# Attention and linear attention on one core: packed odd and even heads for the out-projection, paced projections, inserted zero products, 32-row scores, and transposing loads

## The chip, the cores and the metric

The kernel runs on one core of one Trainium2 chip. The metric is the device time of one execution in microseconds (us). The clock in this text is the share of its full clock that TensorE (PE) was granted. "Fast" and "slow" are states of runs: a run on one core is called slow when it is over 1.5% above the fastest of the same kernel. Ratios are the mean time of one kernel's fast runs over that of the kernel before in the same rounds, so they are not quite ratios of the medians that I quote.

## The reference

Two independent attentions over 2048 tokens, width 512, 32 heads of 16, side by side in the output.

```python
# A: softmax attention
q, k, v = split(x @ wqkv)                        # 32 heads, 16 wide
p = softmax(q @ k^T / 4)                         # 32 x 2048 x 2048
a = (p @ v) @ wo
# B: linear attention
phi(t) = [softmax(t @ w_phi), softmax(-t @ w_phi)]     # 32 features a head
kv, z = phi(k)^T @ v, sum(phi(k));  b = (phi(q) @ kv / (phi(q) @ z + 1e-6)) @ wo
out = concat([a, b], -1)                         # 2048 x 1024, bf16
```

## The kernel before

A is cut into 32 units (8 groups of four heads x 4 chunks of 512 queries), each of 16 key tiles of 128 keys. One key tile of a unit is four score products (K stationary, 512 queries moving, one head per 32-row strip of the PE array), an exponential, and four products with V (one per 32-column strip). ACT does most exponentials. DVE does about a quarter of the key tiles by a bit trick: convert scores to a 16-bit pattern, then three shifted copies, each multiplied with its own scaled V on PE. GpSimd (POOL) does B's elementwise products and the final scaling of each unit.

Each engine's instructions are in a fixed order. A scheduler in the Python source places tasks by a model of their durations and emits that order; on the chip each engine waits on semaphores.

```python
def kq(e, out_ap, u, kt, r):                     # one head's scores
    g, c = units[u]
    n = 16 if g % 2 == 0 else 32                 # rows: even heads 16; odd heads 32, K masked
    return e.matmul(out_ap, KT[32*r:32*r+n, g, kt*128:(kt+1)*128],
                    QT[32*r:32*r+n, c, g//2, :], tile_position=(32*r, 0), ...)
def act_kt(u, kt):    # twice: two kq -> one 128x1024 exponential on ACT; then 4 products with V
    ...
def dve_kt(u, kt):    # twice: two kq -> one 128x1024 conversion on DVE; then 3 adds of 128x2048
    ...               # ad: rg[j] = min(rg[i] + shift_j, 32767), uint16, SBUF to SBUF
# end of a unit: copy the PSUM bank, row sums by DMA, reciprocal, DMA back broadcast,
#   POOL: OT[:, g, :] = X * Yd;  the out-projection multiplies 8 groups with a half-empty WOp
```

All A projections are queued at the start. B's key steps run in PE's gaps by low priority, its query steps after the second chunk of A; what is left runs after A.

Of the kernel before, what the change touches and what calls it, by code (L numbers as in the profile page):

```python
# [124 lines left out]
class _Task:  # L125
    __slots__ = ("eng", "dur", "lat", "deps", "emit", "need", "tok", "end", "res", "then", "rel", "done", "pre",
                 "mode", "rows", "port", "prep")

    def __init__(self, eng, dur, emit, deps=(), lat=0.0, need=(), rel=(), then=None, pre=(), mode="f", rows=(),
                 port=False, prep=None):  # L130
        self.eng = eng
        self.dur = dur
        self.lat = lat
        self.emit = emit
        self.deps = [d for d in deps if d is not None]
        self.need = list(need)
        self.rel = list(rel)
        self.then = then
        self.pre = list(pre)
        self.res = {}  # L140
        self.tok = None
        self.end = None
        self.done = False
        self.mode = mode
        self.rows = rows
        self.port = port
        self.prep = prep


class _Sched:  # L150
# [6 lines left out]
    PE_LAT = 0.26  # L157

    def __init__(self):
# [7 lines left out]
        self.urgent = None  # L167

# [37 lines left out]
    def _choose(self, eng, ss):  # L206
        cand = []
        for s in ss:
            if not s["q"] and s["src"] is not None:
                s["src"](s)  # L210
            if s["q"]:
# [3 lines left out]
                r = self._ready(t)  # L215
# [29 lines left out]

    def _place(self, t, start):
        toks = list(t.pre) + [d.tok for d in t.deps]
# [43 lines left out]
def _main_path(nc, es, P, dsem, flag, A_x, A_wqkv, A_wo, B_x, B_wqkv, B_w_phi, B_wo, out):  # L291
# [4 lines left out]
    NPT = 8  # L296
    NB, NJ = 2, 4
    NR = NB + NJ
    DK = (3, 6, 9, 11, 13, 15)
# [3 lines left out]
    AL, DL, GL = 0.15, 0.15, 0.15  # L303
# [11 lines left out]
    def lin(y):  # L315
# [10 lines left out]
    hmask = sb("hmask", [128, 1], F32)  # L326
# [13 lines left out]
        hmask[:], mask8[:].rearrange("p (r a) -> p a r", a=2)[:, 1:2, :], AX.X, ALU.add), [t_m8])  # L340
# [5 lines left out]
    OT = sb("OT", [128, NG, 512], BF)  # L346
    VP = sb("VP", [128, NKT, VW], BF)
    VJ = sb("VJ", [128, _NPH - 1, len(DK), VW], BF)
    WOp = sb("WOp", [128, NG, 512], BF)
# [6 lines left out]
    OA = sb("OA", [128, 2, 512], BF)  # L356
    scr = nc.dram_tensor("scr", [NU, 4, 512], F32)
# [7 lines left out]
    y_sl = [_Slot(i) for i in range(2)]  # L365
    r_sl = [_Slot(i) for i in range(2)]
# [16 lines left out]
    pe_op = SC.stream("pe", -0.03)  # L383
    ac_ev = SC.stream("act", -0.1)
    ac_xe = SC.stream("act", -0.2)
    ac_ex = SC.stream("act", 0.0)
    ac_b = SC.stream("act", -0.1)
    dv_x = SC.stream("dve", -0.4)
    dv_xe = SC.stream("dve", -0.3)
    dv_ev = SC.stream("dve", -0.2)  # L390
    dv_n = SC.stream("dve", -0.15)
# [3 lines left out]
    po_n = SC.stream("pool", 0.0)  # L395
    po_v = SC.stream("pool", 0.02)
    sp_q = SC.stream("sp", 0.0)
    sp_b = SC.stream("sp", 0.01)
# [28 lines left out]
    xn = rg[:].rearrange("p a b -> p (a b)")[:, 0:8192].bitcast(BF).rearrange("p (s n) -> p s n", n=512)  # L427
    xa_v = A_x[0].rearrange("(st p) n -> p st n", p=128)
    wa_v = A_wqkv.rearrange("(ct p) n -> p ct n", p=128)

    def load(name, fn, us, deps=(), n=1, pre=(), lat=2.0):
        d = dsem(name)
        return put(sp_q, _Task("sp", us, dma(d, lambda e, t, i: fn(e, i), n), deps, lat=lat, pre=pre))

    l_x, l_w = {}, {}

    def load_x(c, lat):
        l_x[c] = load("xa%d" % c, lambda e, i: e.dma_start(xn[:, 4 * c:4 * c + 4, :], xa_v[:, 4 * c:4 * c + 4, :]), 0.6, lat=lat)

    def load_w(p, lat):  # L440
        l_w[p] = load("wa%d" % p, lambda e, i: e.dma_start(
            w[:, :, p * 512:(p + 1) * 512], wa_v[:, :, p * 512:(p + 1) * 512]), 0.6, lat=lat)

    load_x(0, 4.0)
    load_w(1, 6.0)
    load_w(0, 8.0)
    load_w(2, 9.0)
    load_x(1, 10.0)
    load_x(2, 12.0)
    load_x(3, 14.0)  # L450
    t_wo0 = P.op("dve", lambda e: e.memset(WOp[:], 0.0))
    wo_v = A_wo.rearrange("(g r a d) n -> r a d g n", r=4, a=2, d=16)
    l_wo = load("wo", lambda e, i: e.dma_start(
        WOp[32 * (i // 2):32 * (i // 2) + 16, :, :].rearrange("p (g a) n -> p a g n", a=2)[:, i % 2],
        wo_v[i // 2, i % 2]), 4.0, n=8, pre=[t_wo0], lat=8.0)
    t_yd1 = P.op("dve", lambda e: e.memset(Yd[:], 1.0))
    for s in y_sl:
        s.toks = [t_yd1]
    t_vp1 = [P.op("pool", lambda e, kt=kt: e.memset(VP[:, kt, :], 1.0)) for kt in range(NKT)]
    SC.free["pool"] = 8.0  # L460
    SC.free["pe"] = 1.0

    xt_ready = {}
    for c in range(4):
        for h in range(2):
            tp = put(pe_tp, _Task("pe", 0.5, pe_group(8, lambda e, t, i, c=c, h=h: e.transpose(
                PS[:, t.res["b"].idx, :].bitcast(BF)[:, i * 128:(i + 1) * 128],
                xn[:, 4 * c + i % 4, (2 * h + i // 4) * 128:(2 * h + i // 4 + 1) * 128], ident[:, :])),
                [l_x[c]], lat=PL, need=[("b", G, 1, 1)], pre=[t_ident]))
            dst = xT[:, 2 * h:2 * h + 2, c * 512:(c + 1) * 512]  # L470

            def src(t, tp=tp):
                return PS[:, tp.res["b"].idx, :].bitcast(BF).rearrange("p (a n) -> p a n", n=512)
            rel = [lambda tp=tp: [tp.res["b"]]]
            if h == 0 and c == 0:
                ev = put(ac_xe, _Task("act", 1.0, one("act", lambda e, t, dst=dst, src=src: e.activation(
                    dst, src(t), ACT.Copy)), [tp], lat=AL, rel=rel))
            else:
                ev = put(dv_xe, _Task("dve", 0.7, one("dve", lambda e, t, dst=dst, src=src: e.tensor_copy(
                    dst, src(t))), [tp], lat=DL, rel=rel))  # L480
            xt_ready[(c, h)] = ev
            if c == 3:
                for sl in rg_sl:
                    sl.left += 1
                    tp.rel += [sl]
# [13 lines left out]
    def proj(kind, a, c, on_act=False):  # L499
        deps = [l_w["qkv".index(kind)]]  # L500
# [13 lines left out]
        def evac(dst, src, act, pre=()):  # L514
            if act:
                return put(ac_ev, _Task("act", 0.55, one("act", lambda e, t: e.activation(
                    dst, src(), ACT.Copy)), [last], lat=AL, rel=rel, pre=pre))
            return put(dv_ev, _Task("dve", 0.64, one("dve", lambda e, t: e.tensor_copy(dst, src())),
                                    [last], lat=DL, rel=rel, pre=pre))
        if kind == "v":  # L520
# [3 lines left out]
            if a in DK:  # L524
                for j in range(1, _NPH):
                    vj_ready[(a, j)] = put(po_v, _Task("pool", 1.0, one("pool", lambda e, t, j=j: e.tensor_scalar(
# [3 lines left out]
        else:  # L530
            k0 = evac(KT[:, 2 * a, c * 512:(c + 1) * 512], lambda: bank_of(first), on_act)
            k_ready[(2 * a, c)] = k0
            k_ready[(2 * a + 1, c)] = put(dv_ev, _Task("dve", 0.24, one("dve", lambda e, t: e.tensor_scalar(
                KT[:, 2 * a + 1, c * 512:(c + 1) * 512], KT[:, 2 * a, c * 512:(c + 1) * 512], hmask[:, 0:1], None,
                ALU.mult)), [k0], lat=DL, pre=[t_hm], port=True))

    proj("k", 0, 0, True)
    proj("q", 0, 0)
    for c in range(4):
        if c:  # L540
            proj("k", 0, c)
        for kt in range(4 * c, 4 * c + 4):
            proj("v", kt, 0)
    for g in range(1, 4):
        for c in range(4):
            proj("k", g, c)
        proj("q", g, 0)
    for c in range(1, NQC):
        for g in range(4):
            proj("q", g, c)  # L550
# [10 lines left out]
    state = {"ua": 0, "ud": 0}  # L561

    def kq(e, out_ap, u, kt, r):
        g, c = units[u]
        n = 16 if g % 2 == 0 else 32
# [3 lines left out]
    def qk_task(u, kt, half, need, bank):  # L569
        g, c = units[u]  # L570

        def mm(e, t, i):
            return kq(e, PS[:, bank(t, i), :], u, kt, 2 * half + i)
        return _Task("pe", MM, pe_group(2, mm), [q_ready[(g // 2, c)], k_ready[(g, kt // 4)]], lat=PL, need=need,
                     mode="r", rows=(2 * half, 2 * half + 1))

    def pv_task(u, deps, lhs, rhs, rel):
# [13 lines left out]
        t = _Task("pe", MM, emit, deps, lat=PL, rel=rel, mode="c", prep=lambda t: open_pv(t, u))  # L591
# [9 lines left out]

    def close(u):
        left[u] -= 1
        if left[u]:
            return
# [3 lines left out]
    def make_unit_end(u):  # L609
        g, c = units[u]  # L610
        xv = _Task("dve", 0.66, one("dve", lambda e, t: e.tensor_copy(X[:, t.res["x"].idx, :], PS[:, pvb[u].idx, :])),  # L611
# [3 lines left out]
        def after_x(_):  # L615
            xi = xv.res["x"].idx
            d1 = put(sp_q, _Task("sp", 0.5, dma(d_s1[u % 2], lambda e, t, i: e.dma_start(
                sums[:, 16 * u:16 * u + 16], X[16:128:32, xi, :])), [xv], lat=2.2,
# [8 lines left out]
                Yd[32 * r:32 * r + 16, t.res["y"].idx, :],  # L627
                scr[u][r:r + 1, :].broadcast_to([16, 512])), 4), [d2], lat=2.2, need=[("y", y_sl, 1, 1)]))
            mul[u] = put(po_n, _Task("pool", 1.5, one("pool", lambda e, t: e.tensor_tensor(  # L629
                OT[:, g, :], X[:, xi, :], Yd[:, d3.res["y"].idx, :], ALU.mult)), [d3] + op_done.get(c - 1, []), lat=GL,  # L630
                rel=[lambda: [xv.res["x"]], lambda: [d3.res["y"]]], port=True))
# [3 lines left out]

    d_s1 = [dsem("s1a"), dsem("s1b")]
# [6 lines left out]
    def act_kt(u, kt):  # L643
        exps = []
        for half in range(2):
# [4 lines left out]
            def ex_emit(e, t, qk=qk):  # L650
# [3 lines left out]
            exps.append(put(ac_ex, _Task("act", 0.96, one("act", ex_emit), [qk], lat=AL,  # L654
                                         need=[("p", pt_sl, 1, 1)], rel=[lambda qk=qk: [qk.res["A"]]])))
        put(pe_pa, pv_task(u, exps + [v_ready[kt]],
                           lambda h: VP[:, kt, 17 * h:17 * h + 32],
# [4 lines left out]
    def dve_kt(u, kt):  # L662
# [4 lines left out]
        for half in range(2):  # L667
            def bank(t, i):
                return t.res["D"][i].idx
            def rows(t, q0=q0):  # L670
                if q0 is None:
                    t.res["h"] = 0 if max(SC.rows[0:2]) <= max(SC.rows[2:4]) else 1
                else:
                    t.res["h"] = 1 - q0.res["h"]
                t.rows = (2 * t.res["h"], 2 * t.res["h"] + 1)

            def mm(e, t, i):
                return kq(e, PS[:, bank(t, i), :], u, kt, t.rows[i])
            qk = _Task("pe", MM, pe_group(2, mm), [q_ready[(g // 2, c)], k_ready[(g, kt // 4)]], lat=PL,
                       need=[("D", G, 2, 1)] + ([] if q0 else [("i", ri_sl, 1, _NPH)]), mode="r", prep=rows)  # L680
# [1377 lines left out]
```

## Time and profile before

| kernel before | |
|---|---|
| time, median (at the prediction) | 951.43 us (949.11 to 970.63) |
| profiled run | 990.27 us, clock 0.777, a slow one |
| fast runs of later rounds | 942 to 954 us, clock 0.83 to 0.85 |

All stretches and waits of the kernel before are from this slow run.

First the page of the kernel before: busy us and share, then the span in 40 slices (digits are tenths busy; PEclk is the granted clock in tenths), then the two costliest groups (count, busy, mean ns, idle before).

```profile
span 988.5 us, 16687 instructions
...
PE 888.8 (90%) x6997; PEld 237.9 (24%) x7085; DVE 751.2 (76%) x1045; ACT 777.9 (79%) x849; POOL 171.8 (17%) x239
...
PE   7999999989999989999999999999999999999742
...
ACT  3799999766999677878679887878879999999100
...
PEclk9999999555998555656569575858769999899855
...
L652 ACT ACTIVATE pT<-PS 128x1024 bf16<-128x1024 f32 x766 | 739.4, 1031 | 130.3 <-PE PS L566 120.2
L566 PE MATMUL PS<-QT,KT 16*128 16x512 bf16 (+1 forms) x2048 | 385.8, 462 | 18.9 <-ACT pT L652 12.0
```

PE looks 90% busy throughout, while its clock is full for the first seventh, then mostly half.

The table by stretches of the same kernel: busy us of each engine and its instruction count, then clock, DMA share and GB/s.

```profile
core 0: us, PE busy (x) PEld busy (x) DVE busy (x) ACT busy (x) POOL busy (x), PEclk, DMA share, GB/s
40.00:160.00 120.00, 115.53 (x1014) 31.94 (x1029) 113.85 (x154) 117.80 (x127) 12.21 (x13) 1.00 0.03 8
310.00:520.00 210.00, 197.97 (x1469) 41.52 (x1484) 148.58 (x188) 158.62 (x168) 24.91 (x14) 0.59 0.03 7
914.00:988.50 74.50, 33.60 (x161) 15.99 (x163) 29.58 (x77) 7.17 (x13) 26.82 (x64) 0.67 0.08 25
```

At full clock ACT is full (117.8 of 120 us). At clock 0.59 it is busy 158.6 of 210. What it waits for stands in the waits view (who waited for whom: total us, times, longest):

```profile
ACT pT L652 <- PE PS L566: 120.2, 176, 4.6
```

After the last exponential (914 us) 74 us follow. The chain of waits there (start, us, what) repeats every 8 us, one output step of B:

```profile
949.09 0.48 POOL w L991
...
951.01 1.35 POOL w L1006 x3
...
953.01 0.96 PE PS L964 x8
953.97 1.72 PE PS L1021 x4
955.72 0.69 DVE w L1026
...
957.12 0.48 POOL w L991
```

### The profile page before, as it was taken

The page shows a single profiled execution, that of the slowest core. Times are in us where ns is not written, and L with a number is a line of the kernel's source. Part 1 is how long each engine was busy: PE and PEld are TensorE (multiplying, and loading weights), DVE is VectorE, ACT ScalarE, POOL GpSimd, SP SyncE. Part 2 cuts the span into 40 slices and gives each one's busy share as a digit, 9 for nine tenths or more (in the row PEclk, how much of TensorE's full clock was granted, in tenths as well). Part 3 has the DMA queues.
Part 4 walks back from the last instruction along what each step waited for, and adds up shares of the span by engine and source line. Part 5 has one row for each costly group of instructions (what it writes and reads, how often), then busy time and mean ns, then how long its engine had stood idle before and what let it go on. Part 6 is the DMA issues. An engine that isn't in the chain of part 4 may idle for free.

```text
span 988.5 us, 16687 instructions
## 1 busy us (share of the span) xinstructions
PE 888.8 (90%) x6997; PEld 237.9 (24%) x7085; DVE 751.2 (76%) x1045; ACT 777.9 (79%) x849; POOL 171.8 (17%) x239
## 2 busy tenths in 40 slices
PE   7999999989999989999999999999999999999742
PEld 3322222121222112212112222222223222223321
DVE  5799999766699676868649588768779976989443
ACT  3799999766999677878679887878879999999100
POOL 4400000011003020202001102110210402243342
PEclk9999999555998555656569575858769999899855
DMA  6000000700000000000000000000000100000100
GB/s 170 1 8 7 7 8 23 158 11 7 12 18 13 2 7 7 7 1 7 7 12 18 7 7 7 7 7 7 7 11 18 27 10 12 13 12 13 34 21 19
DMA packets 36212, 18.48 MB, mean 19 GB/s; under 512 B 24864, under 2 KB 34080, under 8 KB 36128
## 3 DMA queue, kind: packets, MB, share of 16 engines
q1 hardware_dynamic: 36128, 17.33, 7.3%
q8 instruction: 56, 0.92, 0.4%
q14 instruction: 28, 0.23, 0.1%
HBM read 9.45 MB, written 4.46 MB: 14 GB/s over the span
## 4 chain that ended last, share of the span: by engine, by line
PE 61%; DVE 19%; ACT 13%; POOL 3%; issue 3%; DMA 1%; SPq 0%; POOLq 0%; DVEq 0%
PE PS L581 23%; PE PS L566 23%; ACT pT L652 12%; DVE rg L688 7%; DVE rg L700 6%; PE PS L747 3%; PE PS L508 3%; PE PS L880 2%; PE PS L1021 1%; PE PS L947 1%; PE PS L505 1%; DVE w L976 1%; PE PS L849 1%; DVE w L1026 1%; POOL w L1006 1%
## 5 line engine op out<-in xcount | busy, mean ns | idle before, releaser
L652 ACT ACTIVATE pT<-PS 128x1024 bf16<-128x1024 f32 x766 | 739.4, 1031 | 130.3 <-PE PS L566 120.2
L566 PE MATMUL PS<-QT,KT 16*128 16x512 bf16 (+1 forms) x2048 | 385.8, 462 | 18.9 <-ACT pT L652 12.0
L688 DVE TENSOR_SCALAR rg<-PS 128x1024 uint16<-128x1024 f32 x258 | 313.9, 1217 | 81.6 <-PE PS L566 80.4
L700 DVE TENSOR_SCALAR rg<-rg 128x2048 uint16<-128x2048 uint16 x387 | 270.6, 727 | 19.2 <-PE PS L581 16.7
L581 PE MATMUL PS<-pT,VP 128*32 128x512 bf16 x1532 | 180.6, 468 | 3.7 <-ACT pT L652 3.2
L581 PE MATMUL PS<-rg,VJ 128*32 128x512 f16 x1548 | 177.7, 472 | 5.8 <-DVE rg L700 5.1
L566 PEld LDWEIGHTS PS<-QT,KT 16*128 16x128 bf16 (+1 forms) x2048 | 83.8, 94 | 349.4 <-ACT pT L652 189.0
L629 POOL TENSOR_TENSOR OT<-X,Yd 128x512 bf16<-128x512 f32 x32 | 42.0, 1314 | 346.7 <-DMA Yd<-scr 305.3
L581 PEld LDWEIGHTS PS<-pT,VP 128*32 128x32 bf16 x1532 | 40.4, 97 | 110.2 <-issue 89.6
L869 POOL TENSOR_TENSOR w<-zb,stat 128x1024 bf16<-128x1024 bf16 x16 | 34.4, 2152 | 178.5 <-DVE stat L867 178.5
L991 POOL TENSOR_TENSOR w<-w 128x204 f32<-128x204 f32 (+1 forms) x48 | 31.0, 646 | 190.9 <-DVE w L976 190.8
L581 PE MATMUL PS<-rg,VP 128*32 128x512 f16 x516 | 62.8, 478 | 1.3 <-DVE rg L688 1.0
L581 PEld LDWEIGHTS PS<-rg,VJ 128*32 128x32 bf16 x1548 | 41.1, 101 | 76.4 <-issue 35.7
L1016 ACT ACTIVATE w<-PS 128x512 bf16<-128x512 bf16 x16 | 9.7, 604 | 53.7 <-PE PS L1013 53.6
L747 PE MATMUL PS<-WOp,OT 128*128 128x512 bf16 x113 | 39.4, 452 | 8.7 <-POOL OT L629 5.7
L508 PE MATMUL PS<-xT,w 128*128 128x512 bf16 x111 | 35.5, 400 | 4.3 <-issue 2.1
L947 PE MATMUL PS<-xT,Wfq 128*128 128x512 bf16 x111 | 35.7, 417 | 3.2 <-issue 2.6
L611 DVE COPY X<-PS 128x512 f32<-128x512 f32 x32 | 22.0, 687 | 16.7 <-PE PS L581 10.3
L1013 PE MATMUL PS<-ident,w 128*128 128x128 bf16 x64 | 7.6, 253 | 24.9 <-POOL w L1006 24.6
L973 DVE RECIPROCAL stat<-PS 128x24 f32<-128x24 f32 (+1 forms) x48 | 13.5, 282 | 20.5 <-PE PS L964 20.5
L1006 POOL TENSOR_TENSOR w<-w,den 128x192 bf16<-128x192 f32 (+1 forms) x48 | 25.0, 548 | 14.3 <-DVE den L1001 14.3
L880 PE MATMUL PS<-w,xT 128*128 128x512 bf16 x50 | 23.9, 547 | 4.0 <-issue 3.6
(78 smaller groups left out, 450.8 us busy)
## 6 DMA issues: line engine op xcount, KB each, us to landing
Yd<-scr SPq DMA_DIRECT2D x128, 32.0 KB, 1.8
rg<-in_A_x_dram SPq DMA_DIRECT2D x4, 512.0 KB, 8.3
out_dram<-OA SPq DMA_DIRECT2D x16, 128.0 KB, 1.7
out_dram<-w SPq DMA_DIRECT2D x16, 128.0 KB, 1.7
w<-in_A_wqkv_dram SPq DMA_DIRECT2D x3, 512.0 KB, 6.0
WOp<-in_A_wo_dram SPq DMA_DIRECT2D x8, 64.0 KB, 7.9
sums<-X SPq DMA_DIRECT2D x32, 8.0 KB
scr<-rin SPq DMA_DIRECT2D x32, 8.0 KB, 1.4
```

Source lines behind the costliest of these rows:

```text
L508: return e.matmul(bank_of(t), w[:, ct, c0:c0 + 128], xT[:, ct, c * 512:(c + 1) * 512], start=(ct == 0), stop=(ct == 3))
L566: return e.matmul(out_ap, KT[32 * r:32 * r + n, g, kt * 128:(kt + 1) * 128], QT[32 * r:32 * r + n, c, g // 2, :], start=True, stop=True, t ...
L581: return e.matmul(PS[32 * r:32 * r + 32, pvb[u].idx, :], lhs(8 * (g // 2) + 2 * r + g % 2), rhs(r), start=t.res["first"], stop=t.res["last ...
L629: mul[u] = put(po_n, _Task("pool", 1.5, one("pool", lambda e, t: e.tensor_tensor(OT[:, g, :], X[:, xi, :], Yd[:, d3.res["y"].idx, :], ALU. ...
L652: return e.activation(pT[:, t.res["p"].idx, :], PS[:, b:b + 2, :].rearrange("p a n -> p (a n)"), ACT.Exp, scale=0.25)
L688: return e.tensor_scalar(rg[:, q0.res["i"].idx, 1024 * half:1024 * half + 1024].rearrange("p (a n) -> p a n", n=512), PS[:, b0:b0 + 2, :], ...
L700: ad = put(dv_ad, _Task("dve", 0.62, one("dve", lambda e, t, j=j: e.tensor_scalar(rg[:, t.res["j"].idx, :], rg[:, q0.res["i"].idx, :], flo ...
L747: return e.matmul(bank_of(f), OT[:, g2 + i, st * 128:(st + 1) * 128], WOp[:, g2 + i, :], start=(g2 + i == 0), stop=(g2 + i == NG - 1))
L869: ph = put(po_phi, _Task("pool", 2.3, one("pool", lambda e, t, x0=x0, rd=rd: e.tensor_tensor(w[:, t.res["k"].idx, 0:1024].rearrange("p (g ...
L880: return e.matmul(PS[:, t.res["b"].idx, :], xT[:, ct, st * 128:(st + 1) * 128], w[:, ct, 1024:1536], start=(ct == 0), stop=(ct == 3))
L947: return e.matmul(PS[:, t.res["b"].idx, :], Wfq[:, ct, t8 * 128:(t8 + 1) * 128], xT[:, ct, cq * 512:(cq + 1) * 512], start=(ct == 0), stop ...
L1006: om.append(put(po_y, _Task("pool", 0.5, one("pool", lambda e, t, gi=gi, n=n, d0=d0, o0=o0: e.tensor_tensor(o_b[(o0 or t).res["o"].idx][:, ...
```

## The change

The intent: keep PE at full clock, finish B together with A, and save PE work. In short:

1. Scores always use 32 rows of the array (both parities of K are masked with zeros).
2. A zero-product filler in the scheduler: where its model sees the array filled less than 0.50 over 3.42 us, it puts in four column products with zero weights; below 0.40 even if real work is delayed.
3. A's projections are released one by one over the first 84 of the 512 key tiles (about a sixth), B's steps from 0.24 to 0.95 of them.
4. Odd heads' outputs land in rows 16 to 31 of each strip, so OT packs both parities: out-projection with 4 instead of 8 products a block (one DMA more for each odd unit). B's query features need half the products (the negative sign moves into ACT's scale).
5. DVE's conversions take one PSUM bank (128x512), not two.
6. x and B's weights arrive transposed by DMA; some loads on ACT's queue; first weights in pieces.

```diff
-        n = 16 if g % 2 == 0 else 32
+        n = 32
...
+    def _fill(self, t, start):
+        e = max(self.free["pe"], max(self.rows))
+        back = 0.0 if t.mode == "c" else self.SWITCH
+        x = e if self.mode == "c" else e + self.SWITCH
+        while True:
+            a = self._recent(max(x, start - back))          # filled share of the last 3.42 us
+            late = x + self.MM + back > start
+            if a >= (self.FORCE if late else self.ACTIVE) or not self.filler(x):
+                break
...
+    def filler(x):            # four products, zero weights, into an open accumulation
+            P.op("pe", lambda e, r=r: e.matmul(PS[32*r:32*r+32, pvb[u].idx, :], zer[:],
+                ones..., start=False, stop=False, tile_position=(0, 32 * r)), ...)
...
+            at.append((32 * (g - 1) + 8 + 4 * c, lambda g=g, c=c: proj("k", g, c)))
+    b_steps += [(n / (NU * NKT), fn) for n, fn in sorted(at, ...)]
...
+    B_AT = (0.24, 0.54, 0.95)
+            b_steps.append((B_AT[0] + (B_AT[1] - B_AT[0]) * st / 16, lambda st=st: k_step(st)))
+            at = B_AT[1] + (B_AT[2] - B_AT[1]) * st / 16
...
-            mul[u] = put(po_n, _Task("pool", 1.5, ... OT[:, g, :] = X * Yd ...
+            m = put(po_n, ... OT[:, c % 2, g // 2, :] if even else Oo[...] ...
+            mul[u] = m if even else put(sp_q, ... 4 DMAs: OT[32*r+16:32*r+32, ...] <- Oo ...
...
+        for n in range(4):    # dve_kt: single rows and single banks
+            qk = _Task("pe", MM, pe_group(1, mm), ..., need=[("D", G, 1, 1)] ...
```

## The prediction

> **What bounds the kernel now.** The TensorE clock. The core view gives a mean granted clock of 0.777 over a 988.5 us profiled span. The table by stretches shows two kinds. At full clock (40 to 160 us) ACT is busy 117.8 of 120 us and makes 127 exponentials of 128x1024 while DVE makes 42 score conversions: 84.5 key tiles, 0.70 per us. At a granted clock near 0.59 (310 to 520 us) it is 154 and 54: 104 tiles in 210 us, 0.50 per us; ACT is busy 159 of 210 us and waits for score products (120 us in the waits view). PE looks over 90% busy in both. The clock falls at about 175 us, some 6 us after the last A projection (products of 128 rows); afterwards only row-tiled scores of 16 or 32 rows and column-tiled PV products run. It is full again when B's query products run between them (from 740 us). [...] here PE was hardly idle, so I take it that partly filled products count for less.

> Second, a tail: the last exponential ends near 914 us; some 74 us of B output steps follow, one per 8 us, each a serial PE, DVE, POOL, ACT chain.

> **What the change does.**
> 1. Spreads A projections over the first fifth of the key tiles and B steps from 0.24 to 0.95, and fills low-activity stretches with zero products, some forced. It should hold the clock near 1, on the critical path: 0.50 tiles per us become 0.67 to 0.70. Estimate: 110 to 130 us.
> 2. B ends at 0.95: the tail shrinks from 74 us to about 15 to 20. Part is no gain, since the work moves under the A stage.
> 3. Out-projection 128 to 64 products, B query features 128 to 64 (0.22 us each at full clock, 28 us of PE time, off the ACT path). Repacking DMAs: hidden.
> 4. Even groups' scores with 32 rows: same duration (446 and 477 ns now), more activity.
> 5. DVE conversions of 1024 (1.22 us x2) become 512 x4 (a 512 eviction takes 0.69 us, about 0.61 pitched): equal or slightly dearer.
> 6. Loads by DMA transpose: first exponential at 13.7 us now, about 10 after.

> **Sum.** ACT: about 380 tiles x 2 x 0.908 us (pitch at full clock: 44 exponentials in 40 us) + 50 us of others = 740 us; DVE: 132 x 4.4 + 160 = 740; these balance. With ACT about 95% used, 780; plus 10 us before the first exponential and 15 of tail: 805 us. PE at full clock has about 740 us of issue work by my estimate, so it nearly co-limits, and fillers are not free.

> **Predicted: 802 us, range 768 to 848.** Faster by over 2%: 0.96; within 2%: 0.03; slower: 0.01.

> **What would show it.** Right: mean granted clock above 0.95, ACT over 90% busy from 20 us to near the end, span minus last exponential under 25 us, about 760 exponentials. Wrong: clock at 0.5 for whole stretches between 0.2 and 0.6 of the run; or full clock but ACT under 85% busy, waiting for scores (PE overfilled); or DVE the full engine (over 97%).

> **What would make it wrong.** Zero products may not count as activity; forced ones may cost more than they save; single-row score products and PSUM banks held by interleaved B steps may starve ACT[...].

The 740 us of PE issue work stands without its terms. Counted from the trace of before (products that start within 30 ns of each other are one group), 2346 groups of score, V and 128x512 products at 0.22 us and 1390 changes to or from score products at 0.1 us (both as measured at full clock, below) are some 655 us, without the smaller products: an estimate, of the same order.

## The result, and the profile after

| | before | changed |
|---|---|---|
| median | 950.27 us | 865.09 us |
| range | 946.79 to 970.63 (4 runs) | 852.89 to 866.92 (4 runs) |
| ratio of fast runs | | 0.905, 95% interval 0.894 to 0.916 |
| profiled run | 990.3 us, clock 0.777, slow | 864.2 us, clock 0.936, fast |
| last exponential ends, of the span | 914.0 of 988.5 us | 830.1 of 862.5 us |

It is 9% faster, and 63 us slower than I said, outside my range. The page of the changed kernel, the same lines:

```profile
span 862.5 us, 17084 instructions
...
PE 772.3 (90%) x7061; PEld 230.5 (27%) x7145; DVE 761.7 (88%) x1306; ACT 758.8 (88%) x856; POOL 157.9 (18%) x153
...
PE   8999999996999989989889899988989999898952
...
ACT  6879999876989999899999879997989989999940
...
PEclk9999999987989999799999859997989999999986
```

The clock is mostly full but for single slices at 7 to 9 tenths. DVE and ACT are both 88% busy. The changed kernel's groups (count, busy us, mean ns, idle before, what ended it); L676 are the zero products, 172 products, so 43 groups of four:

```profile
L744 ACT ACTIVATE pT<-PS 128x1024 bf16<-128x1024 f32 x758 | 715.9, 1064 | 58.2 <-PE PS L634 49.2 <-PE PS L649 6.8
L634 PE MATMUL PS<-QT,KT 32*128 32x512 bf16 x2048 | 365.2, 398 | 33.6 <-ACT pT L744 12.9 <-DVE rg L793 6.0 <-DVE rg L782 5.1
L782 DVE TENSOR_SCALAR rg<-PS 128x512 uint16<-128x512 f32 x532 | 340.7, 680 | 23.7 <-PE PS L634 22.8
L793 DVE TENSOR_SCALAR rg<-rg 128x2048 uint16<-128x2048 uint16 x399 | 280.9, 744 | 9.2 <-PE PS L649 8.3 <-PE PS L950 0.6
...
L676 PE MATMUL PS<-ones_t,zer 128*32 128x512 bf16 x172 | 18.2, 421 | 0.0
```

ACT still waits 49 us for scores (120 in the slow profiled run of before). Stretches of the changed kernel (columns as in the table of before):

```profile
60.00:170.00 110.00, 105.90 (x948) 29.98 (x964) 108.50 (x185) 104.84 (x113) 11.61 (x12) 1.00 0.04 9
260.00:340.00 80.00, 74.74 (x750) 21.72 (x751) 76.00 (x131) 80.00 (x93) 13.94 (x9) 1.00 0.07 17
480.00:520.00 40.00, 36.45 (x332) 9.17 (x329) 27.64 (x45) 31.76 (x34) 7.35 (x5) 0.66 0.05 10
830.00:862.50 32.50, 6.75 (x36) 2.46 (x33) 6.82 (x17) 0.11 (x1) 1.26 (x1) 0.67 0.08 26
```

At full clock (260 to 340 us) ACT is busy all the time. From 480 to 520 us the clock is 0.66 and ACT loses 8 of 40 us. The tail, 830 to 862.5 us, is 32 us with all engines almost empty.

**What makes the clock fall and rise here.** The clock records of both traces change only between 1.0 and 0.5, and every stretch before the last is a whole number of steps of 3.413 us (3.413 to 160.426 us in the kernel before, 3.413 to 177.493 us in the changed one). For each step I added up, from the trace, each product's streaming time (about 0.42 ns for each column moved, over the clock at its start: 128x512 products in a row most often start 0.216 us apart at full clock) times its rows/128 times its columns/128, 128x128 being the largest product here. I call this the filled share; it is good to about 0.01. The numbers below are computed from the trace, not a view of the profile.

```text
windows of 3.413 us           kernel before          changed kernel
full clock, stays full        0.32 and more          0.31 and more
full clock, then halved       up to 0.39             up to 0.37
half clock, stays at half     up to 0.75             up to 0.77
half clock, then full         0.64 and more          0.60 and more
mean while full, staying      0.55                   0.54
```

### The profile page after: what moved, and what is told of

Same layout as the page of the kernel before. It is cut to its first block, busy times and chain, and to the rows that moved or that the text cites. A ratio compares the mean times of both kernels' runs of the same rounds, so it can differ in the third digit from the quotient of the medians.

```text
span 862.5 us, 17084 instructions
## 1 busy us (share of the span) xinstructions
PE 772.3 (90%) x7061; PEld 230.5 (27%) x7145; DVE 761.7 (88%) x1306; ACT 758.8 (88%) x856; POOL 157.9 (18%) x153
## 4 chain that ended last, share of the span: by engine, by line
DVE 32%; ACT 31%; PE 25%; issue 6%; SPq 3%; DMA 1%; POOL 1%; POOLq 0%; DVEq 0%; ACTq 0%
ACT pT L744 28%; DVE rg L782 13%; DVE rg L793 11%; PE PS L649 10%; PE PS L634 9%; PE PS L562 2%; SPq L892 1%; ACT e_k L923 1%; PE PS L559 1%; SPq L889 1%; DVE w L1006 1%; DVE X L696 1%; DVE stat L926 1%; PE PS L836 1%; DVE e_k L1042 1%
## 5 line engine op out<-in xcount | busy, mean ns | idle before, releaser
L744 ACT ACTIVATE pT<-PS 128x1024 bf16<-128x1024 f32 x758 | 715.9, 1064 | 58.2 <-PE PS L634 49.2
L634 PE MATMUL PS<-QT,KT 32*128 32x512 bf16 x2048 | 365.2, 398 | 33.6 <-ACT pT L744 12.9
L782 DVE TENSOR_SCALAR rg<-PS 128x512 uint16<-128x512 f32 x532 | 340.7, 680 | 23.7 <-PE PS L634 22.8
L634 PEld LDWEIGHTS PS<-QT,KT 32*128 32x128 bf16 x2048 | 90.0, 91 | 322.9 <-ACT pT L744 187.1
L649 PE MATMUL PS<-rg,VJ 128*32 128x512 f16 x1596 | 153.9, 403 | 12.8 <-DVE rg L793 12.5
L649 PE MATMUL PS<-pT,VP 128*32 128x512 bf16 x1516 | 154.8, 407 | 1.4 <-ACT pT L744 0.7
L931 POOL TENSOR_TENSOR w<-e_k,stat 128x1024 bf16<-128x1024 bf16 x16 | 32.2, 2011 | 167.3 <-PE PS L950 88.3
L1020 POOL TENSOR_TENSOR w<-w 128x544 f32<-128x544 f32 x16 | 23.0, 1440 | 97.0 <-DVE w L1006 97.0
L836 PE MATMUL PS<-WOp,OT 128*128 128x512 bf16 x53 | 17.1, 422 | 14.5 <-DMA OT<-Oo 12.9
L1006 DVE TENSOR_TENSOR w<-PS,stat 128x408 f32<-128x408 f32 (+1 forms) x48 | 25.1, 522 | 0.5
```

What stands on the lines that cost most here:

```text
L634: return e.matmul(out_ap, KT[32 * r:32 * r + n, g, kt * 128:(kt + 1) * 128], QT[32 * r:32 * r + n, c, g // 2, :], start=True, stop=True, t ...
L649: return e.matmul(PS[32 * r:32 * r + 32, pvb[u].idx, :], lhs(8 * (g // 2) + 2 * r + g % 2), rhs(r), start=t.res["first"], stop=t.res["last ...
L744: return e.activation(pT[:, t.res["p"].idx, :], PS[:, b:b + 2, :].rearrange("p a n -> p (a n)"), ACT.Exp, scale=0.25)
L782: return e.tensor_scalar(rg[:, q0.res["i"].idx, 512 * r:512 * r + 512], PS[:, qk.res["D"].idx, :], ya, yb, ALU.mult, ALU.add)
L836: first, t = two_step(pe_op, lambda e, t, p, st=st: e.matmul(bank_of(t), OT[:, c % 2, p, st * 128:(st + 1) * 128], WOp[:, p, :], start=(p ...
L931: ph = put(po_phi, _Task("pool", 1.95, one("pool", lambda e, t: e.tensor_tensor(pk[t.res["k"].idx].rearrange("p (g f) -> p g f", f=16), e_ ...
```

## The experiments

Each is the kernel before or the changed kernel with one edit. All results passed the comparison with the reference. One run of the kernel before took 2878 us, without a known cause; it is not among the fast runs. Medians count slow runs too. The profiled runs of a_nofill, a_fill60, a_bload and a_nopace were slow ones.

| run | median us (runs) | ratio to before, 95% | clock, profiled run |
|---|---|---|---|
| changed kernel | 865.1 (4) | 0.905, 0.894 to 0.916 | 0.936 |
| b_rows32 | 912.8 (5) | 0.963, 0.960 to 0.967 | 0.889 |
| b_fill | 939.0 (4) | 0.989, 0.983 to 0.994 | 0.867 |
| a_rows16 | 918.8 (4) | 0.970, 0.961 to 0.978 | 0.857 |
| a_nofill | 871.2 (4) | 0.912, 0.904 to 0.919 | 0.914 |
| a_fill60 | 901.8 (4) | 0.947, 0.935 to 0.958 | 0.947 |
| a_btail | 883.9 (4) | 0.933, 0.912 to 0.954 | 0.936 |
| a_bearly | 870.3 (4) | 0.917, 0.906 to 0.929 | 0.927 |
| a_nopace | 888.0 (4) | none: its profiled run and two others were slow | 0.915 |
| a_wide | 862.0 (4) | 0.906, 0.896 to 0.917 | 0.947 |
| a_poolsplit | 847.6 (4) | 0.889, 0.879 to 0.900 | 0.943 |
| a_bload | 866.4 (4) | 0.904, 0.890 to 0.919 | 0.931 |
| a_comb | 843.4 (4) | 0.893, 0.881 to 0.904 | 0.969 |
| a_comb_again | 842.7 (6) | 0.890, 0.885 to 0.895 | 0.962 |
| a_comb8 | 837.8 (6) | 0.881, 0.877 to 0.886 | 0.960 |
| a_combnf | 834.9 (6) | 0.880, 0.874 to 0.885 | 0.953 |

An edit can shift the whole fixed order, and where the clock then falls is partly luck; single differences below some 2% are read with that in mind. b_rows32, a_rows16 and a_poolsplit keep PE's, ACT's and DVE's order exactly.

### Which part holds the clock: rows

In the kernel before, all even groups' scores with 32 rows. (The scores are then sums of two heads: the wrong function on purpose. Scores are so small that the output still passed.)

```diff
-        n = 16 if g % 2 == 0 else 32
+        n = 32
```

> The kernel before with one number changed: even groups' score products use 32 rows instead of 16 (wrong result on purpose: two heads' scores are summed; same instructions, order and durations). In the trace of before, the clock halves after a 3.4 us window whose filled share of the array (rows x columns / 128 x 128, times time) falls below about 0.37. Theory 1 (filled rows count): the share rises by about 0.06 where even groups run, fewer drops, mean clock 0.80 to 0.90 instead of 0.777, 900 to 935 us. Theory 2 (only occupied row groups or only busy time count): clock and time as before within 1%.

The other way round, the changed kernel with 16 rows in even groups (right result):

```diff
-        n = 32
+        n = 16 if g % 2 == 0 else 32
```

> The changed kernel with 16-row scores in even groups (right result, same order of instructions). Theory 1 (rows count): more clock drops, mean clock 0.85 to 0.91, 880 to 905 us. Theory 2: as the changed kernel, 853 to 867 us.

The slice line of b_rows32 (granted clock in tenths):

```profile
PEclk9999999978999685778998596889999899999855
```

The same slice line of the changed kernel with 16-row scores (a_rows16):

```profile
PEclk9889999978879979899789579976999897595575
```

Nothing but the number of rows changed: the same instructions, in the same order, with the same counts. b_rows32 gains 34 us by medians; a_rows16 loses 54 us by medians (two of its four runs are slow; 51 us by the means of the fast runs). Theory 1 holds in both (a_rows16 came out slower than the range I gave). Filled rows count for the clock, though the products take no longer (383 ns for 16 rows and 384 for 32, means at full clock, 40 to 160 us of the kernel before). The pair a_rows16 and changed kernel, both profiled in fast runs, also gives a price: half clock before the last exponential was 235.5 against 88.7 us, and the last exponential ended at 870.7 against 830.1 us. That is 40.6/146.8, about 0.28 us per us at half clock.

### Which part holds the clock: zero products

In the kernel before, the scheduler's filler added as in the change, nothing else; in the changed kernel, no filler; and the filler with higher thresholds. The traces hold 276 and 980 zero products, so 69 and 245 groups; the texts on record say 62 and 244.

```diff
# b_fill: _record, _recent, _fill, filler and the areas of the change, in the kernel before
# a_nofill
-    SC.filler = filler
+    SC.filler = None
# a_fill60
-    ACTIVE = 0.50
-    FORCE = 0.40
+    ACTIVE = 0.60
+    FORCE = 0.50
```

> The kernel before with only the zero-product filler of the change added (62 column groups of zero products placed by the same rule). Theory 1 (zero products count as activity and a few of them suffice): mean clock at least 0.90 and 880 to 910 us. Theory 2 (the filler is placed by a model of time that the chip leaves once a wait is longer than modelled, so it helps little): clock 0.78 to 0.85, 930 to 950 us.

> The changed kernel without any zero products (43 groups of four taken out). Theory 1 (they hold the clock): clock 0.85 to 0.90, 880 to 910 us. Theory 2 (the pacing and the rows hold it, the products are few): within 1.5% of the changed kernel, clock 0.92 or more.

> The changed kernel with the filler's two thresholds raised by 0.1 (0.60 and 0.50): 244 groups of zero products instead of 43. Theory 1 (the clock's drops cost most of the miss): clock above 0.97 and 835 to 852 us. Theory 2 (full clock, but 200 more groups of 0.22 us and two mode switches delay scores, PE being nearly full): clock above 0.97 and 860 us or more.

The two mode switches of that text are measured: in the changed kernel at full clock a V group starts 0.318 us after the score products before it (median of 430), score products 0.332 us after a V group (397), and a V group 0.227 us after another (390), so a switch is about 0.1 us.

Zero products do count for the clock. The clock of b_fill, 0.867 against 0.83 to 0.84 in the fast runs of before, doesn't show it alone, since the filler also changed the order of ACT's and DVE's work. The windows of a_fill60 do: before the last exponential, 33 windows that stayed at full clock would have had shares under 0.33, down to 0.08, without the zero products; with them none had. But in b_fill they bought 1.1%. Without them the changed kernel lies within its scatter. With 245 groups it is 4% slower at a clock of 0.947. The groups of a_fill60, the exponentials and the zero products (980 products, 103 us of PE busy time):

```profile
L744 ACT ACTIVATE pT<-PS 128x1024 bf16<-128x1024 f32 x756 | 714.4, 1056 | 86.2 <-PE PS L634 77.2 <-PE PS L649 6.9
...
L676 PE MATMUL PS<-ones_t,zer 128*32 128x512 bf16 x980 | 103.2, 413 | 0.0
```

ACT waits 77 us for scores there against 49 in the changed kernel, and the tail is 60.6 us, since B's query steps were pushed behind the last exponential. So PE has no room for so many of them; this trace is of a slow run, but the fast runs alone give the 4%. That the filler is not worth its place is shown below, on the repaired kernel.

### Pacing and the tail

```diff
# a_btail: some of B's query steps after the last key tile, as before
-    B_AT = (0.24, 0.54, 0.95)
+    B_AT = (0.24, 0.54, 1.30)
# a_bearly: all of B's steps at once
+    B_AT = (0.24, 0.24, 0.24)
# a_nopace: all A projections at once
-    b_steps += [(n / (NU * NKT), fn) for n, fn in ...]
+    b_steps += [(0.0, fn) for n, fn in ...]
```

> The changed kernel with B's query steps spread to 1.30 instead of 0.95 of the key tiles, so that some six of the sixteen run after the last key tile, as in the kernel before. Theory 1 (about half of the gain is the tail that went under the A stage): the tail from the last exponential grows from 32 to 60 to 80 us, the A stage ends 5 to 15 us sooner, the whole is 20 to 40 us slower (885 to 905). Theory 2 (the steps cost the A stage as much as they cost alone, and the gain is all clock): within 1% of the changed kernel.

> The changed kernel with all of B's steps released at 0.24 instead of paced from 0.24 to 0.95. Theory 1 (pacing keeps the full-array products spread, and these hold the clock): the middle third is at full clock, the last third, without B, drops often: clock 0.88 to 0.92, 875 to 900 us. Theory 2 (32-row scores hold the clock; pacing matters little for it): clock within 0.02 of 0.936, time within 1.5%.

> The changed kernel with all A projections released at once instead of spread over the first fifth of the key tiles. Theory 1 (the spread matters): first scores starve, A stage ends 10 us or more later. Theory 2: within 1%.

With B's last steps left over, the A stage ended at 811.7 instead of 830.1 us and the tail grew from 32.4 to 61.3 us. By medians the whole lost 19 us, by the ratios of fast runs 3% (0.933 against 0.905, with intervals that overlap a little): at the low end of what I had put down, or just under it. So shortening the tail by 29 us gives 11 us by the profiles and 19 by the medians: much of the work moved, rather than went. Pacing B for the clock's sake does little (a_bearly, 870 us, clock 0.927). Releasing A's projections at once starves the first scores, as theory 1 said: between 40 and 60 us, at full clock in both runs, ACT is busy 5.2 of 20 us, against 14.0 in the changed kernel. The 23 us by medians hold three slow runs; the only fast one took 872 us, against 853 and 864 of the changed kernel. I have no fast-run ratio for that one, so its size stays open.

### Width of the conversions

The two-bank conversions of the kernel before in the changed kernel.

```diff
-        for n in range(4):     # one row, one bank, 128x512
+        for half in range(2):  # two rows, two banks, 128x1024
```

> The changed kernel with the score conversions of before (two of 1024 columns, each needing two neighbouring PSUM banks) in place of four of 512. Theory 1 (the change of width costs DVE time, 4 x 0.64 against 2 x 1.22 us): a little faster, up to 1%. Theory 2 (a pair of banks is hard to get while projections and B steps take single banks): slower by 1 to 4%, fewer conversions done on DVE.

862 us: no difference that these rounds can see. Fewer conversions (246 of 1024, worth 492 of 512, against 532) were made on DVE, as theory 2 said, but DVE's time per tile was lower, as theory 1 said.

### What still stops PE, and two repairs

Nine drops remain before the last exponential of the changed kernel. In six of them a DVE instruction takes over 1.3 us instead of 0.2 to 0.7. The timeline of the changed kernel around one drop (start, us, engine, line, operation; in brackets the idle time and what ended it):

```profile
434.36 2.96 DVE L793 TENSOR_SCALAR rg<-rg 128x2048 uint16<-128x2048 uint16 x3
...
434.52 1.65 POOL L715 TENSOR_TENSOR Oo<-X,Yd 128x512 bf16<-128x512 f32 x1 [6.50 <-DMA Yd<-scr]
...
435.06 0.09 PEld L634 LDWEIGHTS PS<-QT,KT 32*128 32x128 bf16 x2 [0.47 <-ACT pT L744]
...
436.77 0.09 PEld L634 LDWEIGHTS PS<-QT,KT 32*128 32x128 bf16 x1 [1.62 <-DVE rg L793]
...
438.07 1.02 ACT L744 ACTIVATE pT<-PS 128x1024 bf16<-128x1024 f32 x1 [1.23 <-PE PS L634]
```

Three adds, 0.6 us each, take 2.96 us while a GpSimd product runs (434.52 to 436.17). PE then stands 1.32 us for the add, and ACT 1.23 us for PE. In that window the filled share was 0.29 and the clock halved. Over the trace, 25 of 399 adds last over 1.1 us, each beside a GpSimd instruction that began first, and they end 0.55 us after that instruction ends, whatever its length (1.12 to 2.00 us). An add that overlaps no GpSimd instruction takes 0.68 us (mean of 330), one that does 1.05 us (69). So these adds wait for the GpSimd instruction to end; I call that a lock-out. What makes them wait is not shown.

The first repair issues GpSimd's long products in parts:

```diff
-  one("pool", ... w[128x1024] = e_k * stat)     # 2.0 us
+  parts("pool", 4, ... w[:, 256*i:256*i+256] = ...)
   # likewise the unit's scaling, B's sum and B's last product, in two parts each
```

> The changed kernel with GpSimd's long products (2.0, 1.4, 1.35 and 1.2 us) issued in two or four parts each, nothing else, same order on the other engines. In the changed kernel's trace, before five of eight drops of the clock a 2048-wide DVE add (0.63 us alone) lasts 1.2 to 2 us while a GpSimd product runs, and PE idles behind it. Theory 1 (DVE is locked out for the length of one GpSimd instruction): the adds' mean falls from 0.744 to under 0.69 us, fewer drops, clock above 0.95, 835 to 850 us. Theory 2 ([...] the drops have other causes): adds and time unchanged or worse by GpSimd's overhead.

The adds of a_poolsplit (count, busy us, mean ns):

```profile
L802 DVE TENSOR_SCALAR rg<-rg 128x2048 uint16<-128x2048 uint16 x399 | 273.9, 726 | 9.0 <-PE PS L657 8.4 <-PE PS L959 0.3
```

The same group in the run with the loads alone (a_bload), where the long product was whole:

```profile
L793 DVE TENSOR_SCALAR rg<-rg 128x2048 uint16<-128x2048 uint16 x396 | 289.4, 770 | 12.6 <-PE PS L649 11.6 <-PE PS L950 0.8
```

No add is over 1.26 us any more (2.45 before), but the mean fell only to 726 ns, not below 690 (35 adds last over 1.1 us instead of 25, each held for less long), and there were still nine drops, 75 us at half clock against 89. The gain is 17 us by medians, with overlapping intervals of the ratios (0.889 and 0.905); all four runs lie below all four of the changed kernel, by 1 us at the nearest. The theory's direction holds, its size for the adds does not, and that the long adds cause the drops is not shown: the long ones went, and the number of drops stayed. Besides the drops, the shorter stalls themselves may be part of it; the runs do not separate the two.

The second stop is the queue. The changed kernel's SP queue around 198 us:

```profile
187.09 10.22 SPq L892 DMA_TRANSPOSE xT<-in_B_x_dram  x4
...
201.39 0.60 SPq L702 DMA_DIRECT2D sums<-X  x1
203.83 0.25 DVE L705 RECIPROCAL rin<-sums 128x16 f32<-128x16 f32 x1 [7.12 <-DMA sums<-X]
...
204.69 0.62 PE L649 MATMUL PS<-rg,VJ 128*32 128x512 f16 x4 [6.59 <-DVE rg L793]
...
205.89 1.02 ACT L744 ACTIVATE pT<-PS 128x1024 bf16<-128x1024 f32 x1 [6.95 <-PE PS L634]
```

Four transposing loads hold the queue 10.2 us. A unit's row sums are issued late, DVE waits 7.1 us in place for them, and PE and ACT behind it. The scheduler had booked 2 us for these four loads. The repair books what the trace shows, one task per load:

```diff
-  b_wt = b_load("wt", ..., 8, freed, 18.0)      # one block, 8 x 0.5 us
+  b_wt = [b_load("wt%d" % i, ..., 1, freed, 3.0, 1.3) for i in range(8)]
-  b_x = b_load("xb", ..., 4, freed, 25.0)
+  b_x = [b_load("xb%d" % i, ..., 1, freed, 5.0, 2.56) for i in range(4)]
```

> The changed kernel with B's twelve transposing loads as twelve tasks of their measured issue time (1.3 and 2.56 us) instead of two blocks of 4 and 2 us. In the changed kernel they hold the SP queue for 9.1 and 10.2 us, a unit's sums arrive 7 us late and DVE, PE and ACT all stop. Theory: the stop of 6 to 7 us at 198 to 205 us goes, with the cold stretch after it: 6 to 14 us faster. Rival: the loads end later and the stop moves to B's first steps: no gain.

The stop of 7 us is gone, and the time is the same (866 us). Six of its eight drops had an add of 2.41 us or so beside them: this order met GpSimd's 2 us products more often (the adds' mean is 770 ns, above). So the two repairs together:

> The two repairs together: GpSimd's long products in parts, and B's transposing loads as single tasks. In the run with the loads alone, the stop at 198 us went, yet six of eight drops of the clock followed a 2.41 us add, that is one locked out by a whole 2.0 us GpSimd product. Theory (both causes of drops are real and add): fewer drops than with the parts alone, 830 to 845 us. Rival (where the drops fall is a lottery of the fixed order, and the load repair gives nothing): 845 to 855 us.

843 us, at the upper end of what I expected from both; two drops and 27 us at half clock in the profiled run, whose last exponential ends at 803.5 us. But by the ratios it is no faster than the parts alone (0.893, and 0.890 in the repeat, against 0.889), so a gain from the second repair is not shown and the rival is not excluded. That run was the fastest of four, so I ran it again beside two variants, one without zero products and one with the long product in eight parts:

```diff
# a_combnf, on a_comb
-    SC.filler = filler
+    SC.filler = None
# a_comb8, on a_comb
-  parts("pool", 4, ... 256 columns)
+  parts("pool", 8, ... 128 columns)
```

> The kernel with the two repairs once more, beside the other two on the same chip: 838 to 850 us again, as a measure of what the order of the day is worth; its first profile's clock of 0.969 was the best of its four runs, so 0.95 to 0.97.

> The two repairs together, without any zero products. Without them the changed kernel alone came out within its own scatter (871 against 865 us). Theory 1 (zero products bridge short dips and are worth keeping): at least 1% slower than the repaired kernel with them (843 us), clock under 0.955. Theory 2 (they have no part in the gain): 838 to 848 us.

> The two repairs, with the longest GpSimd product (128x1024, four parts of 0.66 us) in eight parts. In the repaired kernel both remaining drops stand beside adds of 1.21 us, locked out for about one part. Theory 1 (the lock lasts one instruction): the slowest adds fall below 1.1 us, time 835 to 845 us. Theory 2 (GpSimd's overhead per part, about 0.15 us, eats it): 845 us or more.

The overhead per part in the last text can be read from two traces: 128x1024 takes 2.01 us whole in the changed kernel, and its four parts average 0.663 us in a_poolsplit, 2.65 us together, so 0.16 us more a part.

The repaired kernel repeats (842.7 us). Without any zero product it is faster, not slower: 0.880 against 0.890 of before, at a slightly lower clock (0.953 against 0.962). The intervals just touch (0.8852 and 0.8846), but in the same rounds on the same chip all six runs without it (829 to 839 us) lie below all six with it (842 to 851). So the filler is useless here, and most likely a small loss; taking it out also changes the fixed order, and one order was tried. Eight parts give 838 us; the slowest adds stayed at 1.26 us, beside GpSimd's other products, so my mark for theory 1 was not met, and adds over 1.1 us fell from 52 to 25. a_combnf, at 834.9 us, beats both kernels: 12% under the kernel before, 3% under the changed one by the ratios (0.880/0.905). Its page:

```profile
span 834.4 us, 16854 instructions
...
ACT  6889989969989999999998989899999999998960
...
PEclk9999999968989999999997989799999999999995
```

## Why the prediction was wrong

**What bounds the kernel: right.** The clock bounds the kernel before, and partly filled products count for less: rows alone moved the clock from about 0.83 to 0.89.

**"It should hold the clock near 1": the first failed step.** I took 805 us as a sum at full clock. The changed kernel spent 88.7 us at half clock before its last exponential. At the 0.28 us of the rows pair (0.30 between b_rows32 and the profiled run of before, which was a slow run) that is about 25 us, an estimate. What failed is not that zero products don't count; they do. The filler fills by the model's idea of time. The model does keep adds and GpSimd apart (it never lets them overlap), but nothing on the chip holds the two engines to its times, and 25 adds of the changed kernel were held up by a GpSimd instruction after all. The true times of the SP queue it does not have. Six of the nine drops stand beside a long DVE instruction and one beside the queue's stop; that these are their causes is argued, not shown, since cutting GpSimd's products left nine drops. And the way back mostly took a share above 0.7 (8 of 10 returns), which ordinary work at half clock seldom reaches (under a fifth of the windows that stayed at half clock in the kernel before, up to the last exponential). I gave the 110 to 130 us to the filler and the pacing, and no time to the rows. Rows in both directions are worth 34 to 54 us of the 85; the filler nothing that can be seen.

**"15 of tail": mis-sized.** It is 32.4 us, 17 more. The last unit's way out in the changed kernel (start, us):

```profile
831.64 0.69 DVE L696 COPY X<-PS 128x512 f32<-128x512 f32 x1 [0.51 <-PE PS L649]
832.36 0.59 SPq L702 DMA_DIRECT2D sums<-X  x1
...
834.52 0.34 SPq L708 DMA_DIRECT2D scr<-rin  x1
835.94 1.69 SPq L711 DMA_DIRECT2D Yd<-scr  x4
839.07 1.26 POOL L715 TENSOR_TENSOR Oo<-X,Yd 128x512 bf16<-128x512 f32 x1 [16.45 <-DMA Yd<-scr]
840.36 2.47 SPq L720 DMA_DIRECT2D OT<-Oo  x4
...
844.51 5.20 PE L836 MATMUL PS<-WOp,OT 128*128 128x512 bf16 x15 [12.93 <-DMA OT<-Oo]
```

From the copy of the bank to the first out-projection 13 us pass, through a chain of four DMA steps, one of them the new repacking of odd heads. Then four projections, outputs and the range checks take until 853.3 us, and the program's end is 9.1 us after that. The prediction doesn't say what its 15 us hold.

**"780" for the A stage: mis-sized.** 780 and 10 before the first exponential put the last exponential at 790 us. It ended at 830.1; less 25 for the clock, an estimate, it is 805, so about 15 us remain. DVE's sum was 762 us against my 740: its adds averaged 744 ns, where 4.4 us per tile less four conversions of 0.61 leaves about 0.65 us. ACT's sum was 759 against my 740. The first exponential came at 11.7 us, near my 10, but ACT was busy only 43 of the first 60 us. The three terms, 25 + 17 + 15, make 57 of the 60 us between the 802 and the profiled span of 862.5; since the 15 is what was left over, this is no check of the 25.

**The marks and warnings it named: half right.** First exponential 11.7 after 13.7 us. The number of exponentials is 758, as I said (about 760). Clock 0.936 is below my mark of 0.95. ACT's mark, over 90% busy from 20 us to near the end, was met: 746 of the 810 us from 20 to 830, or 92%. The tail is over the 25 us I named. "Single-row score products ... may starve ACT": a_wide says no. "Forced ones may cost more than they save": likely for all zero products on the repaired kernel; forced ones were not tested apart. The slower adds beside GpSimd's work I named as well, but gave them no term in the sum; that was the warning to follow.

**What stays open.** How the 17 us of a_poolsplit divide between fewer half-clock windows and shorter stalls; and what in the changed kernel's remaining 14 us or so of the gain (85 less 52 for less time at half clock and 19 for the tail, all estimates from single edits that need not add up) is due to packing, loads or halved query products, since none of these was run alone. The 52 is about 260 us at half clock in the A stage of a fast run of before (clock 0.835 over 945 us makes 312 us, less some 50 in the tail), less 89, times 0.3.

## What to carry to other kernels

When PE looks busy but its clock is half, look at how much of the array the products fill in each step of the clock's records (3.413 us here), and fill it where it costs no time: rows of zeros in products that run anyway did more here than zero products put between them (3.7% in b_rows32, 1.1% in b_fill). A fixed order is only as good as its model, so look in the trace for the lock-outs and queue times where the chip leaves the model, before adding work that is meant to bridge the stalls. A lock-out that stands in the model, as GpSimd's does here, can still occur on the chip (25 adds of the changed kernel). Here shortening the lock-outs went with some 2%; booking the queue's times alone showed no gain. A prediction built at full clock must add what one stall costs until the clock returns (3 to 27 us at half clock in the changed kernel), not only the stall.
